# A buffer for single middle units, grouped plain copies and a TensorE turn of one weight tile in a fused attention and gated-MLP forward and backward pass

## The chip, the cores and the metric

The kernel runs on one core of a Trainium2 chip. A core has five engines with an instruction stream each: TensorE (PE, with its weight loads shown apart as PEld), VectorE (DVE), ScalarE (ACT), GpSimd (POOL) and SyncE (SP). SP does no arithmetic here. It issues most DMAs, in the order in which they stand in its stream. The metric is the time of one launch on the device, in microseconds, and less is better.

## The reference, cut to what matters

One layer mixes windowed attention and a gated MLP by a learned gate, and the kernel returns the output and the gradients for seven inputs (the eight outputs are out, dx, dwqkv, dwo, dW_gate, dW_up, dW_down and dgate_w).

```python
# S = 2048 rows, D = 512, 32 heads of 16, window 256, F = 1376, all bf16
g = sigmoid((x * gate_w).sum(-1, keepdims=True))
q, k, v = split_heads(x @ wqkv)
p = softmax(where(0 <= i - j < 256, q @ k.T * 16 ** -0.5, -1e9))
a = (p @ v) @ wo
gate, up = x @ W_gate, x @ W_up
b = (relu(gate) * up) @ W_down
out = g * a + (1 - g) * b
# and, for a given grad_out, d(out)/d(x, wqkv, wo, W_gate, W_up, W_down, gate_w)
```

## The kernel before, in words

The kernel has three stages. They follow each other on every engine, and the order of the instructions is written out by hand.

**Stage 1, the MLP (to about 250 us).** The 11 feature blocks (fc) of 128 columns and the 4 row groups (tg) of 512 rows give 44 steps, and the loop of line 410 runs them in a software pipeline. A step computes the gate, up and hidden-gradient products (L330), turns activations by DMA transposes on SP and accumulates weight gradients (L379, L381). The first steps also turn x (`turn_x`, L265) and the scaled output gradient (`turn_db`, L294) on TensorE, through the two PSUM slots with tag "tr". `WdT[fc]` is a tile of W_down, turned by a DMA transpose (`turn_wd`, L219). Its first tile is queued on SP behind the second quarter of x (`load_x(1)`) and ahead of the rest of x and grad_out (lines 243 to 252).

**Stage 2, attention (about 250 to 742 us).** The heads are taken in 4 groups of 8 (c = 0 to 3). A group goes through 16 rows (j) of 128 queries; a row is written (c,j) below. A row has a diagonal key block (role d), a middle one (m, keys of j-1) and a far one (f, keys of j-2). Each is done in two halves of four heads, so that a full row has six units. One unit is one step n of the loop of line 815:

- `front`: the scores ST (L626) on TensorE, the exponential into a bf16 tile on ACT (L635), a mask on POOL.
- `front_dp` and, a step later, `gradp`: the product dPT (L649), then a product on DVE (L654) into the second part of the same tile.
- three steps later, `rowsum`: the sums BA (L663, L665). After the row's last unit ACT copies them to `BAs` (L669, two buffers).
- `flip`: the probabilities are turned. For some units a DMA transpose on SP does it (L682, into p2d or p2m), for the others TensorE (L692).
- `cd_piece`: the products CD (L495, L498) for a key block, from the turned tiles and from `rq`. A list `cdq` holds them until a step that line 865 sets.
- `small_ops`: short POOL operations on `BAs` that make `rq` (five buffers) and, by way of a tile `t1`, the query gradient (L713 to L728).

The diagonal units are turned as a pair of halves from a tile PPd (three buffers). Middle units are turned by DMA as a pair in odd rows of groups 0 to 2. In even rows, and in rows 1 to 9 of group 3, it is a single: half 0 goes by DMA and half 1 by TensorE. Pairs and singles both take their tile from PPm, which has two buffers. In group 3 there are no middle pairs.

```python
u.pair = u.role == "d" or (u.role == "m" and j % 2 == 1 and c < DC - 1)
u.dma = u.pair or (u.role == "m" and half == 0 and (c < DC - 1 or j < 10))
```

Beside the rows, other work is fitted in by a running credit: the projections of the next 512 rows (`project_parts`, L128, L131), the weight gradients of the group before (`grad_parts`, L581), whose results are stored on SP two steps later (L574), and DMA transposes of weights for stage 3 (`turn_w`, L526). `spread` (L477) copies a projected tile zT into `zt` in four DMAs of 64 KB, two at each of two steps, and `tr_rows` (L171) turns zT by DMA. `spill` (L509) writes finished rows of q, k, v and output gradients to DRAM, 8 rows (1 MB) at a time.

**Stage 3, output and dx (742 us to the end).** For each of 16 row blocks TensorE forms the output and dx (L952, L956, L983, L998) and dwo (L933). Operands for two blocks at a time are loaded on SP.

Of the kernel before, what the change touches and what calls it, by code (L numbers as in the profile page):

```python
# [9 lines left out]
ALU = mybir.AluOpType  # L10
AX = mybir.AxisListType
BF = mybir.dt.bfloat16
F32 = mybir.dt.float32
# [9 lines left out]
def kernel(  # L23
# [20 lines left out]
    nc = tc.nc  # L44
# [143 lines left out]
    with ExitStack() as p1, tc.manual_schedule():  # L188
# [28 lines left out]
        def turn_wd(fc):  # L217
            WdT[fc] = fp.tile([P, DC, P], BF, tag="WdT", bufs=2, name="WdT")
            nc.sync.dma_start_transpose(out=WdT[fc][:], in_=B_W_down[start_of(fc):start_of(fc) + P, :])  # L219

        warm = fp.tile([P, TGW], BF, tag="rg", name="warm")
        nc.vector.memset(warm[:], 0.0)
        half = TPG // 2
# [17 lines left out]
            nc.sync.dma_start(Wu_sb[:, :, a:b], Wu_v[:, :, a:b])  # L241

        load_x(1)
        turn_wd(0)
        load_go(0)
        load_x(2)
        load_go(1)
        load_x(3)
# [161 lines left out]
        for n in range(N1 + 8):  # L410
            at = lambda lag: steps[n - lag] if 0 <= n - lag < N1 else None
            if at(0):
                gate(at(0))
                if n + 1 < NTG:
                    turn_x(n + 1)
                up(at(0))
                if n < NTG:
                    gate_col(n)
                    db_rows(n)
                if at(0).tg == 0 and at(0).fc > 0:  # L420
                    turn_wd(at(0).fc)
            if 1 <= n <= NTG:
                turn_db(n - 1)
            if at(2):
                dh(at(2))
            if at(1):
                turn_h(at(1))
            if at(3):
                keep(at(3), (hT_d, at(3).hT[:]))
            if at(4):  # L430
                turn_dgu(at(4))
                keep(at(4), (dgT_d, at(4).dgT), (duT_d, at(4).duT))
            if at(6):
                f = weights(at(6))
                if f is not None:
                    stores[n + 1] = f
            if n in stores:
                stores.pop(n)()
            t = n - DA0
            if t % 2 == 1 and 0 <= t // 2 < NT:  # L440
                make_da(t // 2)
            if t % 2 == 0 and 0 < t // 2 <= NT:
                turn_da(t // 2 - 1)
            if t == 2:
                nc.vector.reduce_sum(par[:, 0:1], par4[:], axis=AX.X)
                nc.vector.tensor_scalar(par[:, 1:2], par[:, 0:1], -1.0, 1.0, op0=ALU.mult, op1=ALU.add)
            if n == NTG + 1:
                nc.scalar.activation(tiny[:], tiny[:], ACT.Exp)
            if t in (NT + 3, 2 * NT + 1):
                i = (t - NT - 3) // (NT - 2)  # L450
                nc.gpsimd.memset(zt[i][:, 0, :, :, :], 0.0)
                nc.vector.memset(zt[i][:, 1, :, :, :], 0.0)
            if n == N1 - 2:
                first = project_parts(*groups[0])
            for _ in range({N1 + 1: 2, N1 + 2: 0}.get(n, 1)):
                if first:
                    first.pop(0)()
            z = n - DA0 - NT - 2
            if z == 0:
                load_w(0)  # L460
            if z % 4 == 3 and 0 < z // 4 + 1 < DC:
                load_w(z // 4 + 1)

    p3 = ctx
    if True:
# [21 lines left out]
        def cd_piece(c, kb, qb, half, last):  # L487
            if (c, kb) not in CDs:
                CDs[(c, kb)] = [ps.tile([P, HG, 2 * Dh], F32, tag="CD", bufs=1, name="CD"), True]
            cd = CDs[(c, kb)]  # L490
            rq = RQ[(c, qb)]
            p2 = P2[(c, qb, kb, half)]
            for hh in range(HH):
                h = 2 * hh + half
                nc.tensor.matmul(cd[0][:, h, :], lhsT=p2[:, 0, hh, :], rhs=rq[:, h, 0:2 * Dh],  # L495
                                 start=cd[1], stop=True, skip_group_check=True)
                cd[1] = False
                nc.tensor.matmul(cd[0][:, h, 0:Dh], lhsT=p2[:, 1, hh, :], rhs=rq[:, h, 2 * Dh:3 * Dh],  # L498
                                 start=False, stop=True, skip_group_check=True)
            if last:  # L500
                nc.scalar.copy(sts[c][:, kb, 1:3, :].rearrange("p a (h d) -> p h a d", h=HG),
                               cd[0][:].rearrange("p h (a d) -> p h a d", a=2))
                if kb == NT // 2 - 1 or (kb == NT - 1 and c == DC - 1):
                    spill(c, kb + 1 - NT // 2)

        def spill(c, t0):
            tsl = slice(t0, t0 + NT // 2)
            eng = nc.gpsimd if (c == DC - 1 and t0 > 0) else nc.sync
            eng.dma_start(dqkvo_d[t0 * P:(t0 + NT // 2) * P, c * 4 * P:(c + 1) * 4 * P].rearrange("(t p) n -> p t n", p=P),  # L509
                          sts[c][:, tsl, :, :].rearrange("p t a n -> p t (a n)"))  # L510

        S2 = {}
        nfull = F // P
# [106 lines left out]
        def front(u):  # L620
            tg, jl = u.j // TPG, u.j % TPG
            z = zt[(u.c * NTG + tg) % ZB]
            KTt = proj[(u.c, u.kb // TPG)][f"K{u.half}"]
            ksl = slice((u.kb % TPG) * P, (u.kb % TPG + 1) * P)
            ST = ps.tile([P, HH, P], F32, tag="M", bufs=4, name="ST")
            nc.tensor.matmul(ST[:], lhsT=KTt[:, ksl], rhs=z[:, 0, :, jl, :], start=True, stop=True)  # L626
            if u.dma:
                if u.half == 0:
                    pairs[(u.c, u.j, u.kb)] = wk.tile([P, 2, 2, HH, P], BF, tag=f"PP{u.role}",
                                                      bufs={"d": 3, "m": 2}[u.role], name=f"PP{u.role}")  # L630
                u.PP = pairs[(u.c, u.j, u.kb)][:, u.half, :, :, :]
                u.Pu, u.Pd = u.PP[:, 0, :, :], u.PP[:, 1, :, :]
            else:
                u.Pu = wk.tile([P, HH, P], BF, tag="Pu", bufs=3, name="Pu")
            nc.scalar.activation(u.Pu[:], ST[:], ACT.Exp)  # L635
            if u.role == "d":
                nc.gpsimd.affine_select(out=u.Pu[:], in_=u.Pu[:], compare_op=ALU.is_ge, fill=0.0, base=0,  # L637
                                        pattern=[[0, HH], [1, P]], channel_multiplier=-1)
            elif u.role == "f":
                nc.gpsimd.affine_select(out=u.Pu[:], in_=u.Pu[:], compare_op=ALU.is_ge, fill=0.0, base=-1,  # L640
                                        pattern=[[0, HH], [-1, P]], channel_multiplier=1)
# [55 lines left out]
        def small_ops(c, j, s):  # L697
# [4 lines left out]
            hd = lambda a: a.rearrange("p (h d) -> p h d", h=HG)  # L702
            rinv = wk.tile([P, HG], F32, tag="rinv", name="rinv")
            ndel = wk.tile([P, HG], F32, tag="ndel", name="ndel")
            rq = wk.tile([P, HG, 3 * Dh], BF, tag="rq", bufs=5, name="rq")
            t1 = wk.tile([P, HG, Dh], F32, tag="t1", name="t1")
            RQ[(c, j)] = rq

            def dve():
# [11 lines left out]
                nc.gpsimd.tensor_tensor(out=hd(rows_st[:, j, 3, :]), in0=BAs[:, :, 17:33], in1=bc(rinv[:], Dh), op=ALU.mult)  # L721

            def pool3():
                nc.gpsimd.tensor_tensor(out=t1[:], in0=BAs[:, :, 0:16], in1=bc(ndel[:], Dh), op=ALU.mult)
                nc.gpsimd.tensor_tensor(out=t1[:], in0=t1[:], in1=BAs[:, :, 34:50], op=ALU.add)

            def pool4():
                nc.gpsimd.tensor_tensor(out=hd(rows_st[:, j, 0, :]), in0=t1[:], in1=bc(rinv[:], Dh), op=ALU.mult)  # L728

            at = (6, 7, 10, 12) if j == 0 else (4, 5, 6, 7)  # L730
            return ((s + 3, "dve", dve),) + tuple((s + a, "pool", f) for a, f in zip(at, (pool1, pool2, pool3, pool4)))
# [54 lines left out]
        with tc.manual_schedule():  # L786
# [14 lines left out]
            def background():  # L801
                f, more = bgq.pop(0)
                store = f()
                if store is not None:
                    ev.setdefault(n + 2, []).append(("dma", store))
                return more

            def pieces():
                nonlocal credit
# [5 lines left out]
            while n <= NU + LAG or ev or cdq or bgq:  # L815
                now = ev.pop(n, [])
                u = units[n] if n < NU else None
                if u is not None:
# [3 lines left out]
                    if u.first and u.j % TPG == 0:  # L822
                        if gi + 1 < len(groups):
                            prq = project_parts(*groups[gi + 1])
                            due = n + sum(2 * min(3, j + 1) for j in range(u.j, u.j + TPG)) - 3
                            if gi + 2 == len(groups):
                                due -= 10
                    if u.first and u.j == 6 and u.c > 0:
                        ev.setdefault(n + 1, []).append(("dma", lambda c=u.c - 1: spill(c, NT // 2)))
                    if u.first and u.j == 1 and u.c > 0:  # L830
                        ready = grad_parts(u.c - 1)
                    if u.first and u.j == TPG - 1 and u.c > 0:
# [18 lines left out]
                if w is not None:  # L851
# [3 lines left out]
                    if w.last:  # L855
# [5 lines left out]
                        for kb in done:  # L861
                            qbs = range(kb, min(NT, kb + 3))
                            for qb in qbs:
                                for half in range(2):
                                    e = n + 1 if qb < w.j else n + 5
                                    cdq.append((e, w.c, kb, qb, half, qb == qbs[-1] and half == 1))
                if u is not None and not (w is not None and w.first):
                    front_dp(u)
# [13 lines left out]
                elif prq and not held and ((credit > 0.4 and n > fed + 1) or due - n <= len(prq)):  # L882
# [2 lines left out]
                    prq.pop(0)()  # L885
                    if len(prq) == 4:
                        for k in range(NP):
                            ev.setdefault(n + 1 + k // 2, []).append(("dma", lambda gi=gi, k=k: spread(gi + 1, k)))
                    if not prq:
                        late += plan.get(gi + 1, [])  # L890
                elif bgq and len(prq) <= 2 and credit > 0.3:
# [149 lines left out]
```

## Time and profile before

| quantity | value |
|---|---|
| times of three runs | 934.29, 937.22 and 938.29 us, median 937.22 |
| the profiled execution | 937.59 us, its span 935.9 us |
| TensorE busy | 910.8 us, 97% of the span |
| VectorE, ScalarE, GpSimd busy | 489.4, 446.6 and 482.7 us, 52%, 48% and 52% |
| granted TensorE clock | 0.998 |
| SP's hardware queue q1 | 142.10 MB, 80.6% of 16 engines' span |
| spills | 7 of 1024 KB on SP, 5.8 us to landing, and one on POOL |
| DMA transposes of probabilities | 64 into p2d (5.5 us to landing), 54 into p2m (4.4 us) |

The profile lists, for each engine, its busy time, groups of instructions and what ended the idle time before them. A line such as "A <- B: 14.2, 11, 2.5" in the view of waits says that A waited for B 14.2 us in total, 11 times, 2.5 us at the longest. In a timeline the columns are start, duration, engine, line and operation, and a bracket at the end holds the idle time before it and what ended it. PE is idle for about 25 us of the span.

### The profile page before, as it was taken

The page shows a single profiled execution, that of the slowest core. Times are in us where ns is not written, and L with a number is a line of the kernel's source. Part 1 is how long each engine was busy: PE and PEld are TensorE (multiplying, and loading weights), DVE is VectorE, ACT ScalarE, POOL GpSimd, SP SyncE. Part 2 cuts the span into 40 slices and gives each one's busy share as a digit, 9 for nine tenths or more (in the row PEclk, how much of TensorE's full clock was granted, in tenths as well). Part 3 has the DMA queues.
Part 4 walks back from the last instruction along what each step waited for, and adds up shares of the span by engine and source line. Part 5 has one row for each costly group of instructions (what it writes and reads, how often), then busy time and mean ns, then how long its engine had stood idle before and what let it go on. Part 6 is the DMA issues. An engine that isn't in the chain of part 4 may idle for free.

```text
span 935.9 us, 26578 instructions
## 1 busy us (share of the span) xinstructions
PE 910.8 (97%) x10873; PEld 576.2 (62%) x10873; DVE 489.4 (52%) x910; ACT 446.6 (48%) x784; POOL 482.7 (52%) x934
## 2 busy tenths in 40 slices
PE   7999999999999999999999999999999999999998
PEld 4565656555657776677676677667777644444443
DVE  4433344333377777667676676766677322222223
ACT  5422232222368777567776677766688211111111
POOL 1554545445267777666677567666667411111111
PEclk9999999999999999999999999999999999999999
DMA  9988889999798999998999789999999599778731
GB/s 264 212 194 186 195 177 221 206 220 197 165 166 140 163 194 164 145 177 145 183 170 169 162 131 200 158 173 163 172 183 193 147 272 225 186 186 189 186 93 46
DMA packets 485043, 166.49 MB, mean 178 GB/s; under 512 B 409720, under 2 KB 483672, under 8 KB 484920
## 3 DMA queue, kind: packets, MB, share of 16 engines
q1 hardware_dynamic: 462568, 142.10, 80.6%
q10 hardware_dynamic: 20592, 17.57, 6.8%
q0 software_dynamic: 1760, 5.11, 1.6%
q8 instruction: 85, 1.39, 0.6%
q14 instruction: 38, 0.31, 0.1%
HBM read 32.15 MB, written 36.24 MB: 73 GB/s over the span
## 4 chain that ended last, share of the span: by engine, by line
PE 79%; DMA 7%; POOL 5%; ACT 5%; DVE 2%; issue 1%; SPq 0%; POOLq 0%; ACTq 0%; DVEq 0%
PE wps L379 8%; PE dxps L983 7%; PE ST L626 6%; PE dPT L649 6%; PE pt L692 5%; PE dxps L998 4%; DMA p2m<-PPm 4%; PE wps L581 4%; PE dps L381 4%; PE dhps L330 4%; PE ups L330 4%; PE gps L330 4%; PE bps L952 4%; PE CD L495 3%; PE pp L128 3%; PE BA L663 3%
## 5 line engine op out<-in xcount | busy, mean ns | idle before, releaser
L637 POOL TENSOR_SCALAR_AFFINE_SELECT PPd<-PPd 128x512 bf16<-128x512 bf16 x128 | 81.2, 634 | 128.9 <-ACT PPd L635 127.9
L654 DVE TENSOR_TENSOR Pd<-Pu,dPT 128x512 bf16<-128x512 bf16 x154 | 104.0, 679 | 73.4 <-POOL Pu L640 72.3
L626 PE MATMUL ST<-z,K 128*128 128x512 bf16 x360 | 136.5, 379 | 5.5 <-ACT PPm L635 3.3
L649 PE MATMUL dPT<-z,V 128*128 128x512 bf16 x360 | 136.9, 380 | 3.0 <-ACT PPm L635 2.1
L344 POOL TENSOR_TENSOR hT<-rg,upm 128x512 bf16<-128x512 bf16 x44 | 52.2, 1186 | 119.6 <-DVE upm L342 85.0
L635 ACT ACTIVATE Pu<-ST 128x512 bf16<-128x512 f32 x154 | 92.6, 601 | 43.8 <-PE ST L626 42.8
L379 PE MATMUL wps<-dgu_r,x_r 128*128 128x256 bf16 (+1 forms) x704 | 103.9, 270 | 0.5 <-DVE wst L74 0.5
L654 DVE TENSOR_TENSOR PPd<-PPd,dPT 128x512 bf16<-128x512 bf16 x128 | 87.3, 682 | 19.9 <-POOL PPd L637 18.0
L635 ACT ACTIVATE PPd<-ST 128x512 bf16<-128x512 f32 x128 | 77.3, 604 | 23.1 <-PE ST L626 20.6
L379 PEld LDWEIGHTS <-x_r 128*128 128x128 bf16 x704 | 68.3, 98 | 31.2 <-issue 0.8
L640 POOL TENSOR_SCALAR_AFFINE_SELECT Pu<-Pu 128x512 bf16<-128x512 bf16 x112 | 71.7, 640 | 22.3 <-ACT Pu L635 21.3
L961 ACT COPY a_sb<-aps 128x512 f32<-128x512 f32 x16 | 9.4, 586 | 152.9 <-issue 137.7
L342 DVE SCALAR_TENSOR_TENSOR upm<-rg,ups 128x512 bf16<-128x512 bf16 x44 | 30.2, 685 | 85.6 <-ACT rg L336 45.8
L336 ACT ACTIVATE rg<-gps 128x512 bf16<-128x512 f32 x44 | 26.3, 598 | 93.9 <-PE gps L330 22.0
L381 PE MATMUL dps<-db_r,h_r 128*128 128x512 bf16 x176 | 66.8, 379 | 0.0
L635 ACT ACTIVATE PPm<-ST 128x512 bf16<-128x512 f32 x78 | 47.1, 604 | 32.3 <-PE ST L626 15.9
L354 POOL TENSOR_TENSOR dgu<-dh_sb,rg 128x512 bf16<-128x512 bf16 x44 | 56.5, 1285 | 8.0 <-ACT dh_sb L350 7.0
L692 PE MATMUL pt<-ident,Pd 128*128 128x128 bf16 x616 | 59.9, 220 | 0.0
L692 PE MATMUL pt<-ident,Pu 128*128 128x128 bf16 x616 | 59.4, 218 | 0.0
L654 DVE TENSOR_TENSOR PPm<-PPm,dPT 128x512 bf16<-128x512 bf16 x78 | 52.6, 674 | 5.6 <-ACT PPm L635 4.3
L967 POOL DMA_DIRECT2D out_dram<-o_sb x16 | 8.7, 542 | 90.7 <-DVE o_sb L965 90.7
L72 ACT COPY p<-pt 128x1024 bf16<-128x1024 bf16 x51 | 52.4, 1028 | 1.3
(172 smaller groups left out, 2361.5 us busy)
## 6 DMA issues: line engine op xcount, KB each, us to landing
dqkvo_d<-rows_st SPq DMA_DIRECT2D x7, 1024.0 KB, 5.8
hT_d<-hT ACTq DMA_DIRECT2D x44, 128.0 KB, 2.5
dgT_d<-dgu ACTq DMA_DIRECT2D x44, 128.0 KB, 2.9
duT_d<-dgu ACTq DMA_DIRECT2D x44, 128.0 KB, 3.1
duT_g<-duT_d SPq DMA_DIRECT2D x8, 640.0 KB, 5.7
gt<-hT_d SPq DMA_DIRECT2D x7, 640.0 KB, 5.4
dgT_g<-dgT_d SPq DMA_DIRECT2D x7, 640.0 KB, 5.2
z<-zT SPq DMA_DIRECT2D x60, 64.0 KB, 2.2
```

What stands on the lines that cost most here:

```text
L330: nc.tensor.matmul(out[:], lhsT=w(c), rhs=x(c), start=(c == 0), stop=(c == DC - 1))
L354: nc.gpsimd.tensor_tensor(out=k.duT, in0=dh_sb[:], in1=k.rg[:], op=ALU.mult)
L379: nc.tensor.matmul(acc["w"][:, c, 0:2 * nw], lhsT=x_r[:, t, c * P:(c + 1) * P], rhs=k.dgu_r[:, :, i, s0:P], start=(go_ and c % 2 == 0), st ...
L381: nc.tensor.matmul(acc["d"][:], lhsT=k.h_r[:, i, :], rhs=db_r[:, t, :], start=go_, stop=no_)
L626: nc.tensor.matmul(ST[:], lhsT=KTt[:, ksl], rhs=z[:, 0, :, jl, :], start=True, stop=True)
L635: nc.scalar.activation(u.Pu[:], ST[:], ACT.Exp)
L637: nc.gpsimd.affine_select(out=u.Pu[:], in_=u.Pu[:], compare_op=ALU.is_ge, fill=0.0, base=0, pattern=[[0, HH], [1, P]], channel_multiplier=-1)
L640: nc.gpsimd.affine_select(out=u.Pu[:], in_=u.Pu[:], compare_op=ALU.is_ge, fill=0.0, base=-1, pattern=[[0, HH], [-1, P]], channel_multiplier=1)
L649: nc.tensor.matmul(u.dPT[:], lhsT=VTt[:, ksl], rhs=z[:, 1, :, jl, :], start=True, stop=True)
L654: nc.vector.tensor_tensor(out=u.Pd[:], in0=u.Pu[:], in1=u.dPT[:], op=ALU.mult)
L692: nc.tensor.transpose(pt[:, a, hh, :], src[:, hh, :], ident[:])
L983: nc.tensor.matmul(dxps[:], lhsT=src[:, fc, lsl], rhs=W6[(wt, fc)], start=(i == 0), stop=(i == nmm - 1))
```

## The change

- **Singles.** Middle pairs keep PPm with its two buffers. A middle single takes a tile of half the size with a tag of its own, PPs, which has one buffer, in all four head groups.
- **Room for it.** `t1` goes away: the query gradient is formed in place in `BAs`, so a `BAs` buffer is held until the last POOL operation of its row. `rq` has four buffers instead of five.
- **Plain copies.** The four copies of `spread` are issued at one step. Stores of weight gradients and spills wait in a list `copies` until more than two are there or until the copies of `spread` have been issued, and then go out together. Spills are of 4 rows (512 KB). In head group 3 a spill goes out at once, and the very last one on POOL's queue.
- **CD.** In rows 9 to 15 of head group 3 the last pieces of a key block are due six steps after the row's sums, not five.
- **First W_down tile.** Tile 0 of W_down is loaded by a plain DMA behind the first quarter of grad_out, turned by four TensorE transposes into a "tr" slot in step 1 and copied out by DVE. The DMA transpose ahead of grad_out is gone.

```diff
+        wd0 = fp.tile([P, D], BF, tag="dst", bufs=2, name="wd0")
+        def turn_wd0():
+            WdT[0] = fp.tile([P, DC, P], BF, tag="WdT", bufs=2, name="WdT")
+            pt = ps1.tile([P, DC, 2, P], BF, tag="tr", bufs=2, name="ptw")
+            for c in range(DC):
+                nc.tensor.transpose(pt[:, c, 0, :], wd0[:, c * P:(c + 1) * P], ident[:])
+            nc.vector.tensor_copy(WdT[0][:], pt[:, :, 0, :])
...
         load_x(1)
-        turn_wd(0)
         load_go(0)
+        nc.sync.dma_start(wd0[:], B_W_down[0:P, :])
...
+                if n == 1:
+                    turn_wd0()
             if 1 <= n <= NTG:
                 turn_db(n - 1)
...
-                if kb == NT // 2 - 1 or (kb == NT - 1 and c == DC - 1):
-                    spill(c, kb + 1 - NT // 2)
+                if kb % TPG == TPG - 1:
+                    sp = lambda: spill(c, kb + 1 - TPG)
+                    if c == DC - 1:
+                        sp()
+                    elif kb < NT - 1:
+                        copies.append(sp)
+                    else:
+                        ends.append(sp)
...
-                    pairs[(u.c, u.j, u.kb)] = wk.tile([P, 2, 2, HH, P], BF, tag=f"PP{u.role}",
-                                                      bufs={"d": 3, "m": 2}[u.role], name=f"PP{u.role}")
+                    nh, tag, bufs = (2, f"PP{u.role}", {"d": 3, "m": 2}[u.role]) if u.pair else (1, "PPs", 1)
+                    pairs[(u.c, u.j, u.kb)] = wk.tile([P, nh, 2, HH, P], BF, tag=tag, bufs=bufs, name=tag)
...
-            rq = wk.tile([P, HG, 3 * Dh], BF, tag="rq", bufs=5, name="rq")
-            t1 = wk.tile([P, HG, Dh], F32, tag="t1", name="t1")
+            rq = wk.tile([P, HG, 3 * Dh], BF, tag="rq", bufs=4, name="rq")
...
-                nc.gpsimd.tensor_tensor(out=t1[:], in0=t1[:], in1=BAs[:, :, 34:50], op=ALU.add)
+                nc.gpsimd.tensor_tensor(out=BAs[:, :, 0:16], in0=BAs[:, :, 0:16], in1=BAs[:, :, 34:50], op=ALU.add)
...
-                    ev.setdefault(n + 2, []).append(("dma", store))
+                    copies.append(store)
+                    if len(copies) > 2 or gi + 2 >= len(groups):
+                        ev.setdefault(n + 2, []).append(("dma", flush))
...
+            def flush():
+                while copies:
+                    copies.pop(0)()
...
-                    if u.first and u.j == 6 and u.c > 0:
-                        ev.setdefault(n + 1, []).append(("dma", lambda c=u.c - 1: spill(c, NT // 2)))
+                    if u.first and u.j == TPG and ends:
+                        copies.append(ends.pop(0))
...
-                                    e = n + 1 if qb < w.j else n + 5
+                                    e = n + (1 if qb < w.j else 6 if w.c == DC - 1 and w.j > 8 else 5)
...
-                            ev.setdefault(n + 1 + k // 2, []).append(("dma", lambda gi=gi, k=k: spread(gi + 1, k)))
+                            ev.setdefault(n + 1, []).append(("dma", lambda gi=gi, k=k: spread(gi + 1, k)))
+                        ev.setdefault(n + 1, []).append(("dma", flush))
```

In SP's stream of the changed kernel, head group 3 begins with p2d (2,15), p2d (3,0), four copies z, a spill of 512 KB, the single p2m (3,1), rows, p2d (3,1) and p2m (3,2). Before it was p2d (2,15), p2d (3,0), two copies z, p2m (3,1), rows, two copies z, p2d (3,1), p2m (3,2).

## The prediction

> **What bounds the kernel now.** I read the page first, for the engine that sets the end.
>
> ```profile
> span 935.9 us, 26578 instructions
> PE 910.8 (97%) x10873; PEld 576.2 (62%) x10873; DVE 489.4 (52%) x910; ACT 446.6 (48%) x784; POOL 482.7 (52%) x934
> DMA  9988889999798999998999789999999599778731
> ```
>
> TensorE works through 910.8 of 935.9 us at full clock, and the edits take no matmul from it. So what can be won is idle time of PE, 25.1 us, of which the ends of the launch hold several. What can be lost has no such limit. The third line says where a loss could come from: the DMA engines are nine tenths busy through most of attention (slices 11 to 31).
>
> Second, the view of waits for PE, over attention to 560 us, from there to 690 us, from 690 to 760 us, and before 245 us.
>
> ```profile
> PE ST L626 <- ACT PPm L635: 3.1, 3, 2.0
> PE wps L581 <- ACT PPm L635: 1.3, 1, 1.3
> ```
> ```profile
> PE dPT L649 <- ACT PPm L635: 2.1, 2, 1.8
> PE ST L626 <- ACT PPd L635: 0.9, 1, 0.9
> PE ST L626 <- ACT PPm L635: 0.2, 1, 0.2
> ```
> ```profile
> PE CD L495 <- POOL rq L719: 2.6, 6, 0.9
> PE dxps L983 <- DMA duT_g<-duT_d: 0.6, 1, 0.6
> ```
> ```profile
> PE ptx L265 <- DMA x_r<-in_A_x_dram: 2.4, 2, 1.6
> PE ptx L265 <- DVE db_T L74: 0.9, 1, 0.9
> ```
>
> These are the targets: 4.4 us up to 560 us and 2.3 us after it behind the middle exponential, 2.6 us behind `rq`, 2.4 us behind x at the start. Third, the same view for ACT over the whole run says what holds the exponential, and it is a DMA that must first read the old tile.
>
> ```profile
> ACT PPm L635 <- DMA p2m<-PPm: 14.2, 11, 2.5
> ```
>
> ACT waits 14.2 us in 11 waits and PE idles 6.7 us for it. So about 0.7 us of each such wait is absorbed by PE's lead.
>
> Fourth, the timelines of ACT and of SP in head group 3, and the landing of the single issued at 618.51.
>
> ```profile
> 613.70 0.60 ACT L635 ACTIVATE PPm<-ST 128x512 bf16<-128x512 f32 x1 [0.37 <-PE BA L665]
> 622.93 0.60 ACT L635 ACTIVATE PPm<-ST 128x512 bf16<-128x512 f32 x1 [0.23 <-PE ST L626]
> ```
> ```profile
> 611.89 4.45 SPq L682 DMA_TRANSPOSE p2d<-PPd  x2
> 616.44 1.98 SPq L477 DMA_DIRECT2D z<-zT  x2
> 618.51 1.28 SPq L682 DMA_TRANSPOSE p2m<-PPm  x1
> ```
> ```profile
> DMA to landing us min/median/max: 3.3/3.3/3.3
> ```
>
> The first two lines are the exponentials that open rows (3,2) and (3,3). The single of row (3,1) is issued at 618.51 and lands 3.3 us later, at 621.8, which is 8.1 us after (3,2) has opened. With two buffers that harms nobody. With one buffer, (3,2) may not open before 621.8.
>
> Last, the view of DMA queues from 560 to 622 us, to see if that landing could come sooner.
>
> ```profile
> DMA packets 39854, 11.23 MB, mean 181 GB/s; under 512 B 38433, under 2 KB 39841, under 8 KB 39841
> q1 hardware_dynamic: 39841, 11.06, 109.4%
> ```
>
> SP's queue holds all 16 engines for the whole of these 62 us (packets overlap, hence 109%). It is full, and it moves 11.06 MB / 62 us = 0.178 MB per us.
>
> **The change part by part.** All sums are against the profiled execution, 937.59 us (span 935.9 and 1.7 around it), which lies 0.4 us above the median of 937.22.
>
> *Pairs keep PPm.* A pair is reused four rows later instead of two. Rows take 6 to 10 us and a p2m lands 8.9 us after issue at worst, so these waits go. Up to 560 us that is 4.4 us off PE.
>
> *Singles in groups 0 to 2.* One buffer reused two rows later is the distance of before: no cost. Their landings come 2 to 10 us before the reuse in nearly all rows, and one wait of 0.4 us (1,12) stays.
>
> *Singles in group 3.* Here a single is made in every row, so the distance falls from two rows to one. In a full queue the landing of p2m (3,1) is set by the bytes ahead of it. Between 560 us and that landing, before has one spill of 1 MB and after has two of 512 KB, and after has two more z copies ahead: 0.13 MB / 0.178 = 0.7 us. So it lands at 622.5, less the shift of all that came earlier, and (3,2) opens then instead of at 613.70: 8.8 us later. PE's lead absorbs 0.7, and PE's wait behind PPd (0.9, at 618) does not come on top, which leaves 7.2. The 2.3 us of PPm waits after 560 us vanish in this: whatever PE gains there it waits out here. Grouping may let the queue switch less between copies and transposes. No row prices that. Between 0 and 2 us I take 1, by the landing of z, z, rows, z, z at 583.6 to 590.2, where 0.5 MB take longer than the 2.8 us of the mean rate. So +6.2 us, with ends of +2 and +9. Behind the blocked exponential on ACT stand the copies of turned tiles, of BA and of CD. PE runs on only until its four score slots are taken, so it stops within two units.
>
> *Rows (3,3) to (3,9).* In before, singles land 4.7, 2.8, 3.6, 2.3 and 0.7 us after the opening of the next row in rows 3, 4, 5, 6 and 8. But that is the backlog, and the long wait works it off: a row needs p2d, p2m and two weight turns, 40 tiles of 32 KB or 1.3 MB, 7.4 us of queue in rows of 9.3 us. What remains are rows with copies in front of the single. At (3,5) two stores, a spill, p2d, four z and rows stand ahead of it. I take +2, between 0 and +6.
>
> *CD one step later.* Five of the six waits for `rq` are in rows 10 to 14 (0.24 four times and 0.69), the last is in the drain. A step is 1.2 us, more than any of them: -1.7 (ends 0 and -2.6).
>
> *The place of t1.* `BAs` of row 0 is now held to its last POOL operation. In group 2 that ends at 504.3 (L728), while ACT copies `BAs` of row 2 at 503.1. ACT waits 1.2 us, and PE, whose next BA stood at 504.56, sees at least 0.2 and at most 1.2 us. Three groups (the fourth is inside the long wait): +1.0. `rq` with four buffers: a buffer is read until two rows later, so it is free in time, 0.
>
> *First W_down tile.* The windows of DMA show 45 GB/s between 8.0 and 9.5 us, when the transpose is under way, and 326 GB/s right after it:
>
> ```profile
> 8.00:9.50 1.50, 0.72 (x13) 0.72 (x14) 0.06 (x1) 0.60 (x1) 0.00 (x0) 1.00 1.27 45
> 9.50:17.00 7.50, 5.94 (x85) 4.05 (x83) 4.59 (x9) 4.81 (x8) 1.81 (x2) 1.00 1.05 326
> ```
>
> Without it x and grad_out land some 2 us sooner, and the 2.4 us behind x go. Added are four transposes of 0.07 us on PE (16 take 1.07) and one copy on DVE of about 0.45 us (128x512 from PSUM takes 0.40 to 0.48), and the second turn of the first output gradient needs the slot that this copy frees. The copy stands behind two scalings (1.53 us), so PE waits there for more than the 0.9 us that it waited for db_T. I take -1.5, between -2.4 and +0.3.
>
> *Other copies.* The last spill is 512 KB on POOL's queue instead of 1 MB, so duT_g comes earlier: -0.6. On SP a group of copies takes 0.6 us each to issue, 3 us in a row; except in group 3 they have two rows of slack.
>
> The Trainium skill's page "DMA: Bandwidth & Descriptors", section "Rules for kernel authors", speaks against smaller spills: it wants at least 1 MiB per DMA for bandwidth, and calls transfers under 64 KB mostly overhead. The rows here half agree: 640 KB land in 5.2 to 5.7 us and 1024 KB in 5.8. If a half spill held the full queue as long as a whole one, the sum would be some 3 us higher; by bytes it is as above.
>
> Sum: -4.4 + 6.2 + 2 - 1.7 + 1.0 - 1.5 - 0.6 = +1.0. That is 938.6 against the profiled execution, 938.2 on the scale of the median, and I forecast 938.
>
> **The rivals.** *The single buffer holds every row (slower).* The queue doesn't recover, because p2m (3,j) always stands behind p2d (3,j-1) and two weight turns. For it: the five landings above, late by 14.1 us in all. Five waits less 0.7 us each give 10.6 instead of 2: 947. Against it: the queue's demand of 7.4 us a row. It decides from about 6 us of waits after (3,2), where the total passes 941.9. That half spills hold the queue like whole ones leads to the same place, 941.
>
> *The queue runs ahead (faster).* If grouped copies spare the queue 2 us per group, three groups before p2m (3,1) bring it 6 us forward instead of 1, and the long wait shrinks to about 1 us: 933; with no waits after it, 931. For it: within the 62 us slices fall to 61 to 86 GB/s between slices of 290. Against it: nothing shows that the switch is what empties them.
>
> *The start wins nothing*, since DVE's copy takes the place of the wait: 939.5, still no change.
>
> **How the numbers follow.** A measurement of this kernel can tell about 0.5%, 4.7 us, from no change. My sum has 0.40, and its own range is 934 to 942. The slower rival has 0.34 and the faster one 0.26. These are also the chances of the three signs: faster 0.26, same 0.40, slower 0.34. For 8 times in 10 the range is 930 to 948.
>
> **What would show it.** In the changed kernel: no wait of ACT for p2m<-PPm worth naming; one wait of ACT for p2m<-PPs of 8 to 13 us near 605 to 618 us, with PE idle for most of it; no wait for `rq` in rows 10 to 14; x no longer waited for at 12 us. The prediction is wrong if PE has no hole at the opening of (3,2), or if PPs waits follow in most rows of group 3 and add up to over 6 us.

## The result, and the profile after

Six executions of the changed kernel took 946.43 to 950.21 us, median 947.23; the kernel before took 935.75 in the same comparison. The ratio is 1.0129, 95% interval 1.0100 to 1.0158: slower by 1.3%. It lies inside the stated range of 930 to 948, at its upper end, where the slower rival stood (947). The forecast of 938 was 9.2 us too low, and the sign was wrong with it: 0.40 had been given to no change and 0.34 to slower.

The profiled execution took 946.43 us, 8.84 more than that of before. It is the fastest of its six, and that of before (937.59) lies near the top of its range (932.97 to 938.33), so the two traces hold 8.8 of the 11.5 us between the medians. The page's heads, its row for TensorE and its row of granted clock:

```profile
span 944.7 us, 26622 instructions
PE 912.2 (97%) x10877; PEld 576.7 (61%) x10877; DVE 492.6 (52%) x911; ACT 448.8 (48%) x784; POOL 481.9 (51%) x934
PE   8999999999999999999999999689999899999998
PEclk9999999999999999999999999889999999999999
```

TensorE is busy 912.2 us instead of 910.8, and the clock has two digits of 8 (slices 26 and 27), where before it had none below 9. (A digit stands for 23 us, and a short stretch at half clock can hide in a 9: before has one, shown further down.) The hole is the 6 of TensorE's row, slice 26, 590 to 614 us. The view of waits for TensorE from 560 to 690 us, and for ACT in the same stretch, name it:

```profile
PE dPT L667 <- ACT PPs L653: 13.6, 3, 10.2
```
```profile
ACT PPs L653 <- DMA p2m<-PPs: 20.2, 4, 12.1
```

The waits for PPm (4.4 and 2.3 us of TensorE before) are gone. One wait of 10.2 us stands in their place, and two more of 2.8 and 0.6. The timeline of ACT shows the two long ones, at the opening of rows (3,2) and (3,3):

```profile
615.07 0.60 ACT L653 ACTIVATE PPs<-ST 128x512 bf16<-128x512 f32 x1 [12.08 <-DMA p2m<-PPs]
627.56 0.60 ACT L653 ACTIVATE PPs<-ST 128x512 bf16<-128x512 f32 x1 [4.50 <-DMA p2m<-PPs]
```

The timeline of SP shows what stands ahead of the single of row (3,1), issued at 611.04. It lands 4.0 us later, at 615.0, and there the exponential starts:

```profile
601.51 6.15 SPq L700 DMA_TRANSPOSE p2d<-PPd  x2
607.75 2.54 SPq L488 DMA_DIRECT2D z<-zT  x4
610.34 0.59 SPq L527 DMA_DIRECT2D dqkvo_d<-rows_st  x1
611.04 1.71 SPq L700 DMA_TRANSPOSE p2m<-PPs  x1
```

**Where the time went.** The 360 dPT products (L649 before, L667 after) stand in the same order in both timelines, so subtracting their starts gives TensorE's lead or lag at each unit.

| at the product of | before, us | after, us | difference | change since the row above |
|---|---|---|---|---|
| first unit of attention | 251.52 | 248.99 | -2.53 | -2.53 |
| opening of (2,11) | 567.21 | 560.35 | -6.87 | -4.34 |
| opening of (3,2) | 613.54 | 603.21 | -10.34 | -3.47 |
| two units later | 616.52 | 617.22 | +0.70 | +11.04 |
| opening of (3,3) | 623.38 | 623.75 | +0.37 | -0.33 |
| near the end of (3,3) | 629.88 | 634.72 | +4.84 | +4.47 |
| last unit of (3,6) | 658.85 | 664.91 | +6.06 | +1.22 |
| opening of (3,11) | 692.95 | 699.01 | +6.06 | 0.00 |
| last unit of all | 728.26 | 736.76 | +8.50 | +2.44 |
| end of the span | 935.87 | 944.73 | +8.86 | +0.36 |

So TensorE was first 10.3 us ahead. It lost 16.4 in rows (3,2) to (3,6), and another 2.4 in the last rows. Not all of the lead is the change's: the version with two buffers below has the same start and came to attention at 251.52 us, no sooner than before.

**The clock.** Idle TensorE does not explain all of the 16.4. The view of windows, with the stretches cut at the ends of the two holes (after the engines' busy times come granted clock, DMA share and GB/s):

```profile
605.50:608.50 3.00, 0.00 (x0) 0.00 (x0) 0.00 (x0) 0.00 (x0) 0.00 (x0) 1.00 1.14 132
608.50:615.70 7.20, 0.00 (x0) 0.00 (x0) 0.00 (x0) 0.63 (x2) 0.00 (x0) 0.52 0.90 208
615.70:618.80 3.10, 3.08 (x38) 1.70 (x38) 2.40 (x5) 2.37 (x5) 1.94 (x5) 0.50 0.00 0
618.80:625.40 6.60, 6.58 (x120) 4.81 (x119) 4.57 (x10) 3.52 (x6) 5.39 (x16) 0.98 0.89 103
628.20:629.60 1.40, 1.40 (x15) 0.90 (x15) 0.67 (x1) 0.79 (x3) 0.61 (x2) 0.88 1.19 215
629.60:632.70 3.10, 3.10 (x19) 1.83 (x17) 1.49 (x3) 1.93 (x3) 1.40 (x4) 0.50 0.84 157
```

The clock falls to half 3.3 us after TensorE stopped (605.5) and stays there until 3.3 us after it took up work again (615.7). After the second hole (625.4 to 628.2) it falls again, for another 3.4 us (629.3 to 632.7). In these stretches a dPT product takes 586 to 634 ns instead of 378. Half of 3.3 and of 3.4 us, 3.3 us in all, is lost on top of the idle time. With the waits of 13.6 and 0.3 us, and less the 0.9 that before waited at 618 us, that makes 16.3 of the 16.4. The Trainium skill's page "TensorE: Matmul & The Clock Gate", section "Part 1: The HAM clock gate (the "warmup" mystery)", says that the array runs at half rate after an idle window of about 3.4 us and recovers after a busy one of that length, by a window that runs freely. The stretches of 3.3 and 3.4 us here agree. That the whole window must be idle does not hold here: the second hole lasted 2.8 us (see the last section).

### The profile page after: what moved, and what is told of

Its sections match the earlier page's. It is cut to its first block, busy times and chain, and to the rows that moved or that the text cites. A ratio compares the mean times of both kernels' runs of the same rounds, so it can differ in the third digit from the quotient of the medians.

```text
span 944.7 us, 26622 instructions
## 1 busy us (share of the span) xinstructions
PE 912.2 (97%) x10877; PEld 576.7 (61%) x10877; DVE 492.6 (52%) x911; ACT 448.8 (48%) x784; POOL 481.9 (51%) x934
## 4 chain that ended last, share of the span: by engine, by line
PE 82%; POOL 5%; ACT 4%; DMA 3%; DVE 2%; issue 2%; SPq 1%; POOLq 0%; ACTq 0%; DVEq 0%
PE wps L388 8%; PE dxps L1007 8%; PE ST L644 7%; PE dPT L667 6%; PE pt L710 5%; PE dxps L1022 4%; PE wps L599 4%; PE dhps L339 4%; PE dps L390 4%; PE ups L339 4%; PE gps L339 4%; PE bps L976 4%; PE pp L128 4%; PE CD L506 3%; PE BA L681 3%; PE CD L509 2%
## 5 line engine op out<-in xcount | busy, mean ns | idle before, releaser
L667 PE MATMUL dPT<-z,V 128*128 128x512 bf16 x360 | 136.8, 380 | 14.6 <-ACT PPs L653 13.6
L681 PE MATMUL BA<-KV,Pu 128*128 128x33 bf16 x616 | 51.1, 178 | 0.5 <-POOL Pu L658 0.5
L599 PE MATMUL wps<-rows_st,x_r 128*128 128x384 bf16 x256 | 50.8, 328 | 0.3 <-DVE Pd L672 0.3
```

Source lines behind the costliest of these rows:

```text
L599: nc.tensor.matmul(wps[:], lhsT=x_r[:, t, part * P:(part + 1) * P], rhs=sts[c][:, t, 0:3, :], start=first and t == t0, stop=last and t == ...
L667: nc.tensor.matmul(u.dPT[:], lhsT=VTt[:, ksl], rhs=z[:, 1, :, jl, :], start=True, stop=True)
L681: nc.tensor.matmul(BA[:, h, 0:33], lhsT=u.Pu[:, hh, :], rhs=kv[:, u.kb % TPG, h, 1:34], start=(u.first and hh == 0), stop=True, skip_group ...
```

## Experiments

Ratios are to the kernel before, run in the same comparison. Versions that ran in different comparisons are set against each other by their ratios. The changed kernel itself has 1.0129 (1.0100 to 1.0158).

**Two buffers for the singles of head group 3.**

```diff
-  nh, tag, bufs = (2, f"PP{u.role}", {"d": 3, "m": 2}[u.role]) if u.pair else (1, "PPs", 1)
+  nh, tag, bufs = (2, f"PP{u.role}", {"d": 3, "m": 2}[u.role]) if u.pair or u.c == DC - 1 else (1, "PPs", 1)
```

> The changed kernel, except that singles of head group 3 take their tile from PPm (two buffers, which no pair needs in that group) and no longer from PPs (one buffer). Groups 0 to 2 are as changed. Theory A, the one buffer makes the long wait, and the wait makes the slow clock behind it: no wait of ACT for p2m in head group 3 worth naming, no idle time of TensorE over 2 us between 600 and 660 us, granted clock 1.00 there. TensorE, which in the changed kernel is 10.3 us ahead of the kernel before at the opening of row (3,2), keeps about 9.4 us of that (it then waits 0.9 us for p2d as before), loses the 2.8 us that the changed kernel loses from row (3,10) on, and ends 6 to 7 us ahead: 929 to 930 us, ratio to before 0.993. Rival B, SP's queue is late for everything in this stretch and the wait moves to PPd or to the CD products: 937 to 942 us. Rival C, the wait is not due to the buffer: 947 us as the changed kernel.

Measured: 936.84 us, ratio 1.0019 (1.0003 to 1.0035). The second buffer takes off 1.1% of the 1.3, but the 929 to 930 us did not come. The hole of row (3,2) is gone. Another one stands at the opening of row (3,3), which now waits for the same single of row (3,1):

```profile
PE ST L644 <- ACT PPm L653: 3.8, 1, 3.8
```
```profile
ACT PPm L653 <- DMA p2m<-PPm: 5.1, 1, 5.1
```

It lands at 619.2 (issue 612.62, 6.6 us), and with the slow clock (0.66 from 620 to 625 us) the hole costs 5.5 us. (The profiled execution, 939.01 us, is the slowest of twelve, so the trace shows the worst case.) So the single buffer is the cause of most of the loss (theory A), and under it lies a second limit: with the queue as it is, a TensorE 8 us ahead has no landing in time even with two buffers. The time fell between A and B, at the edge of B.

**CD at five steps again.**

```diff
-  e = n + (1 if qb < w.j else 6 if w.c == DC - 1 and w.j > 8 else 5)
+  e = n + 1 if qb < w.j else n + 5
```

> The changed kernel with the CD products of the last rows of head group 3 five steps after the row's sums, as before, and not six. By the prediction the later step takes 1.7 us of waits for rq away, so that undoing it gives 949 us and the waits for rq of 0.24 us in rows 10 to 14 come back. Rival, by the trace of the changed kernel, in which TensorE falls 2.8 us behind from row (3,10) on and waits for the products of DVE (0.59 us four times and 1.05 once): the later CD causes these, and undoing it gives 944.5 us.

Measured: 944.98 us, ratio 1.0111 (1.0086 to 1.0136). The medians differ by 2.2 us, but the intervals overlap; the trace is clearer, though it is of the slowest of the four executions (948.21 us, 3.7 us later than the changed kernel when attention begins). From row (3,11) to the last unit TensorE loses nothing against the kernel before, where the changed kernel loses 2.4 us. The view of waits for TensorE from 690 to 760 us, first of the changed kernel, then of this one:

```profile
PE ST L644 <- DVE Pd L672: 3.4, 5, 1.0
```
```profile
PE CD L506 <- POOL rq L736: 2.6, 6, 0.9
```

The later CD does remove the waits for `rq`, as predicted. But no other work takes the place of the CD products that leave the step, so TensorE comes to the next score product earlier and waits there for the slot that a DVE product frees: 3.4 us, and 1.0 more in the drain, instead of 2.6. The rival holds.

**The first W_down tile by DMA again.**

```diff
+        turn_wd(0)
         load_go(0)
-        nc.sync.dma_start(wd0[:], B_W_down[0:P, :])
...
-                if n == 1:
-                    turn_wd0()
```

> The changed kernel with the first W_down tile turned by the DMA transpose of before. Theory A, the end of the long wait is set by SP's queue and not by TensorE: TensorE comes to attention about 2 us later, the wait at the opening of row (3,2) is 2 us shorter, p2m (3,1) lands at the same 615.0 us within 0.7, and the time is the changed kernel's 947.2 within 1 us. Rival B, the queue starts what it does as TensorE releases it, so everything shifts: p2m (3,1) lands 2 us later and the time is 949.3 us.

Measured: 948.03 us, ratio 1.0140 (1.0114 to 1.0166), the changed kernel's time. TensorE comes to attention 1.0 us later, is 0.7 us later at row (3,2), and the hole is 10.1 us. What the old start cost, 1.0 us, is less than two executions of one kernel differ by, so this run does not decide between A and B. The trace of the version above, with CD at five steps, does: its stream is the same up to row (3,9), TensorE is 3.8 us later at row (3,2), the single is issued 3.7 us later (614.72), and the hole is still 10.2 us. The queue's work moves with TensorE's, as B has it.

**Copies, stores and spills ungrouped.** `spread`, the stores and the spills of 1 MB are issued where the kernel before has them; the single buffer stays.

> The changed kernel with the copies of projected tiles, the stores of weight gradients and the spills issued as before (two and two copies, each store two steps after its piece, spills of 1 MB). The single buffer stays. Theory A, the bytes ahead of p2m (3,1) set the end of the long wait: two copies less stand ahead of it, so it lands 0.4 to 1 us sooner, the wait stays at 10 to 12 us, and the time is 946 to 948 us. Rival B, the four copies and the half spill that grouping puts ahead of p2m (3,1) make the wait: it lands 3 us or more sooner, the wait is under 9 us, 944 us or less. Rival C, grouping had brought the queue forward: it lands 2 us or more later, 949 us or more.

Measured: 947.80 us, ratio 1.0138 (1.0115 to 1.0161). The single lands at 617.2 instead of 615.0, of which 1.5 us lie in a later start of attention. TensorE's hole there is 7.2 us, after one of 2.2 us on PPd a row earlier, which brought a slow clock of its own (half from 605.95 to 609.36 us). From the opening of (3,1) to that of (3,4) TensorE loses 14.8 us here and 15.0 in the changed kernel. The time is A's; neither B nor C: the grouping did not make the loss, and it did not bring the landing forward by the 6 us that the faster rival of the prediction needed.

**Weight transposes held back, single buffer kept.**

```diff
+                wait = u is not None and (u.c, u.j) > (DC - 2, 11) and (u.c, u.j) < (DC - 1, 4)
-                if late and (u is None or n % 3 == 1):
+                if late and not wait and (u is None or n % 3 == 1):
```

> The changed kernel, single buffer and all, but no DMA transpose of a stage 3 weight is issued from row (2,12) to row (3,3); the four that stood there, and those behind them, follow from row (3,4) on. In the trace of the changed kernel with two singles these four take SP's queue 6.3 us to issue (1.24, 1.53, 2.18 and 1.31 us). Theory A, the backlog of SP's queue sets the end of the long wait: p2m (3,1) lands 5 to 6 us sooner, at 609 to 610 us, TensorE's hole at the opening of row (3,2) falls from 10.2 to 4 to 5 us, the slow clock behind it goes in part: 938 to 941 us. Rival B, the wait is set by the chain of p2d (2,15), p2d (3,0), the copies and the single, each as long as it is: the hole shrinks by 2 us at most, 945 us. Rival C, the turns that come later make waits of their own in rows 4 to 9: 947 us or more.

Measured: 949.40 us, ratio 1.0161 (1.0132 to 1.0189). The queue has room now: SP issues p2m (2,15) at 596.3, 2.7 us earlier than in the changed kernel, and stands idle in between. The wait stays all the same. The timeline of SP:

```profile
597.82 6.84 SPq L700 DMA_TRANSPOSE p2d<-PPd  x2
604.71 2.91 SPq L488 DMA_DIRECT2D z<-zT  x4
607.66 1.39 SPq L527 DMA_DIRECT2D dqkvo_d<-rows_st  x1
609.17 1.68 SPq L700 DMA_TRANSPOSE p2m<-PPs  x1
```

The single's product is finished at 603.2, but it stands behind the p2d of row (3,0), four copies and a spill, and lands at 613.2, 1.8 us sooner than in the changed kernel. The hole is 6.6 us instead of 10.2, and half of that difference comes from TensorE being 1.7 us later there. That is B for the landing. Rows (3,3), (3,6) and (3,8) bring waits of 2.4, 2.8 and 0.9 us, where the changed kernel has 2.8, 0.6 and none: that is C for the time. (The intervals of the two ratios overlap, so it is no slower than the changed kernel for certain.) With one buffer a row apart, a full queue isn't needed: the order in it is enough.

**All three edits together, and two of them.** Two buffers, CD at five steps, weight transposes held back; then the same without holding them back.

> Three edits to the changed kernel at once: singles of head group 3 from PPm (two buffers), CD in the last rows five steps after the sums, and no weight transposes from row (2,12) to row (3,3). Theory A, the wait of 5.1 us at the opening of row (3,3) with two buffers is the backlog of SP's queue: it goes, TensorE keeps 8 to 10 us of its lead to row (3,10) and to the end, no slow clock: 926 to 929 us, ratio 0.990 to 0.993. Rival B, the transposes held back return as waits in rows 4 to 9 or as late operands of stage 3: 932 to 936 us, a hole of 2 us or more between 630 and 760 us.

> The version with three edits without the third: two buffers for the singles of head group 3, CD at five steps, weight transposes where the changed kernel has them. If the edits add up, the 2.2 us that CD at five steps gave the changed kernel come off the 936.8 us of the version with two buffers alone: 934.6 us, and the hole of 3.9 us at the opening of row (3,3) with its slow clock is there. Then holding the transposes back is worth 8 us on top of the second buffer. Rival: the hole moves with chance by the order in SP's queue, 928 to 931 us.

Measured: 926.45 us, ratio 0.9908 (0.9886 to 0.9930), and 932.43 us, ratio 0.9970 (0.9957 to 0.9983). Both beat both kernels. The page of the first, and a line of its view of waits for ACT:

```profile
span 925.0 us, 26520 instructions
PEclk9999999999999999999999999999999999999999
```
```profile
ACT PPm L653 <- DMA p2m<-PPm: 1.5, 1, 1.5
```

TensorE is 9.3 us ahead of the kernel before at row (3,2), 10.1 at row (3,11) and 10.9 at the end. Without holding back, the hole at (3,3) is 2.9 us, the clock is at half from 619.8 to 623.2 us, and the lead falls from 8.8 to 4.3 us. Holding the transposes back is worth 0.62% (5.8 us, not the 8 expected) with two buffers and nothing with one. The 932.43 us lie between the two expectations of that version.

**Held back in the kernel before, alone.**

> The kernel before with only one edit: no weight transposes from row (2,12) to row (3,3). Theory A, from row (2,13) on the middle exponentials of before wait because SP's queue is late, and not because PPm is short: the waits of TensorE after 590 us (1.8, 0.28, 0.92 and 0.2 us) go, 932 to 933 us, ratio 0.996 to 0.997. Rival B, they are due to the buffer or to the row's own transposes alone: no change, 935.5 us.

Measured: 931.84 us, ratio 0.9968 (0.9953 to 0.9983), as theory A said. The waits of 1.8, 0.28, 0.92 and 0.2 us after 590 us are gone, those of 2.1, 1.3 and 0.5 us up to 560 us stay. So the last ones came from a late queue. The earlier ones are gone in the changed kernel, where pairs have PPm to themselves: they came from the short PPm. What the rest of the change adds, with two buffers and CD at five steps, is the difference to 0.9908, 0.6%.

**Rows (3,1) and (3,2) turned on TensorE, with CD at five steps.** The edit beside that of CD:

```diff
-  u.dma = u.pair or (u.role == "m" and half == 0 and (c < DC - 1 or j < 10))
+  u.dma = u.pair or (u.role == "m" and half == 0 and (c < DC - 1 or 2 < j < 10))
```

> The changed kernel with CD at five steps, and with the middle units of rows (3,1) and (3,2) turned on TensorE as in rows 10 to 15, so that the first single of head group 3 is that of row (3,3). The single buffer stays, and so do the weight transposes. Theory A: the hole at the opening of row (3,2) goes. TensorE does 16 transposes more (0.5 to 1 us for each of two units). If the queue is still late, row (3,4) waits for p2m (3,3) by 1 to 5 us: 929 to 934 us. Rival B, PPd takes its place, since p2d of rows 15 and 0 is in the same queue: waits of ACT for p2d of 3 us or more at rows (3,2) or (3,3), 936 us or more.

Measured: 931.90 us, ratio 0.9980 (0.9961 to 0.9999), against 1.0111 with CD at five steps alone. No hole of 0.4 us or more is left between 560 and 690 us, though the single buffer is in use from row 3 on. ACT still waits 4.9 us for p2m in two waits, little enough for TensorE's lead to absorb most. Its profiled execution is the fastest of ten (928.51), so the trace shows the best case.

**Useless work in the holes.**

```diff
+        FILL = {(DC - 1, 2, "f", 0): 130, (DC - 1, 3, "f", 0): 30}
...
+            m = FILL.get((u.c, u.j, u.role, u.half))
+            if m:
+                pf = psr.tile([P, 2, HH, P], BF, tag="TR", name="pf")
+                for i in range(m):
+                    nc.tensor.transpose(pf[:, i % 2, i // 2 % HH, :], ident[:], ident[:])
```

> The changed kernel with useless TensorE transposes of the identity put into its two holes, 130 ahead of the dPT product that waits 10.2 us in row (3,2) and 30 ahead of the one that waits 2.8 us in row (3,3). At 16 in 1.07 us they take about 8.7 and 2.0 us, less than the holes, so they delay nothing if the holes are as long. Theory A, the idle time itself brings the slow clock (0.5 for about 3.7 us from 615.3 us on, and again from 629.4 to 632.6 us): the granted clock stays 1.00 through both, and TensorE is 2 to 3.5 us earlier at row (3,4) for the same landing of p2m (3,1): 944 to 945 us. Rival B, the clock falls for another reason: no change or, by the added work, 947 to 949 us.

Measured: 951.92 us, ratio 1.0167 (1.0135 to 1.0200). The 130 transposes took 7 us and left a hole of 4.4, after which the clock fell all the same (0.74 from 622.4 to 629 us). Around the second place 0.8 us of idle time was left, the clock stayed at 1.00, and TensorE made up 1.9 us against the changed kernel. So the second half of theory A is borne out, the first was not tried long enough. Why the median is 4.7 us above the changed kernel's stays open. In the trace, which is of the slowest of the four executions, 4.7 us were already missing when attention began, before any of this work: 2.1 of them are a wait for a DVE copy that ends at 203.3 us, and 1.7 the half clock behind it, from 203.2 to 206.6 us. So the total says little about either theory.

**What grouping and the new start are worth without the hole.** The version with all three edits, once ungrouped, once with the old start.

> The version with three edits (two buffers for the singles of head group 3, CD at five steps, weight transposes held back), with copies, stores and spills issued as before. It tells what the grouping is worth when no long wait covers it. Theory A, the grouping moves bytes a little and saves nothing: 926 to 928 us, ratio 0.990 to 0.992. Rival B, the grouping is what keeps the waits behind p2m away: waits of ACT for p2m of 3 us or more come back, 930 us or more. Rival C, the grouped copies cost: 924 us or less.

> The version with three edits, with the first W_down tile turned by DMA as before. It tells what the turn on TensorE is worth when no long wait covers it. By the prediction 1.5 us: 928 us. Rival, by the trace of the changed kernel with the old start, in which TensorE came to attention 1.0 us later: 927.4 us. Rival, nothing, since the wait for the DVE copy of 1.6 us takes the place of those removed: 926.4 us.

Measured: 928.64 us, ratio 0.9933 (0.9913 to 0.9954), and 926.50 us, ratio 0.9908 (0.9888 to 0.9928). The grouping seems to win about 2 us: the ratios 0.9933 and 0.9908 have overlapping intervals, but in one comparison the six executions with it (and the old start) end at 927.08 us and the six without begin at 927.58. None of the three expectations had that. In the traces of the ungrouped version and the one with all three edits, attention is alike to 0.6 us; 2.2 us appear only after its last unit, where the granted clock of the ungrouped one is 0.68 from 720 to 725 us and that of the other 1.00. Whether the grouping or chance sets that off stays open. The new start shows no worth (0.9908 with either start).

## Why the prediction was right or wrong

The trace came out at +8.9 us where the sum had +1.0. Of these 7.9 us, 4.1 lie in the term for CD, 3.7 in that for rows (3,3) to (3,9), 1.0 in the long wait and 1.0 in stage 3; the terms up to 560 us came out 2.0 better than forecast.

- *Pairs keep PPm, -4.4.* Right, but low. After 560 us the lead grows by 3.5, where 2.3 were expected; as predicted, that went into the hole. To (2,11) it grows by 4.3 us against a loss of 1.3 to `BAs`, so 5.7. What the sum lacks is a slow clock in the kernel before: its longest wait for PPm, 1.97 us up to 268.3, is followed by 3.4 us at half clock, and with the wait that goes too (1.7 us). The windows of before:

```profile
265.19:268.60 3.41, 1.44 (x23) 0.92 (x22) 2.75 (x6) 0.86 (x2) 3.21 (x10) 1.00 1.28 148
268.60:272.01 3.41, 3.41 (x32) 2.04 (x31) 1.72 (x4) 2.69 (x5) 2.29 (x5) 0.50 1.16 225
```
- *The long wait, +6.2.* Right, and closely. By the terms of the sum TensorE should have been 1.3 us behind the kernel before when the hole was over (-4.4, -1.5, +1.0, +6.2); at the opening of (3,3) it was 0.4 behind. The single landed at 615.0, where 622.5 less the shift of 4.9 and the 1 us for grouping gives 616.6. That the two ends meet so well is partly luck: TensorE came to row (2,11) 2.0 us further ahead than the sum has it, and from there to (3,3) lost 7.2 us and not 6.2.
- *Rows (3,3) to (3,9), +2.* This step failed. From the opening of (3,3) to row (3,11) TensorE lost 5.7 us. The waits were 2.8 and 0.6 us, not far above the expected sum: the long wait did work the backlog off, so the slower rival's five waits did not come, though its time did. What was missing is the clock, 1.7 us in these rows and as much in the work just before them. The prediction reads TensorE as running "at full clock" from a mean of 0.998; the two lines above, of a hole of 2 us in the kernel before, show the slow clock that a hole of 8 us had to be priced with.
- *CD one step later, -1.7.* Wrong in sign, and the largest miss: +2.4 by the trace. The wait for `rq` did go, but I named no work that would fill its place and did not ask what TensorE would wait for next.
- *The place of t1, +1.0.* The sum was nearly right: ACT has three waits, 2.4 us in all, of which TensorE felt only the first, 1.3 us at 266 us. So the size came from one wait and not from three. Waits of TensorE from 245 to 560 us:

```profile
PE BA L681 <- ACT BAs L687: 1.3, 1, 1.3
```

- *First W_down tile, -1.5.* Wrong. The rival "the start wins nothing" is what the old start in the version with all three edits shows (ratio 0.9908 with either). The wait for x shrinks from 2.4 to 0.9 us, and TensorE waits 1.6 us for the DVE copy. Even the smaller wait for x is in part chance: it is 0.8 and 1.1 us in the two traces with the old start, and 0.4 to 1.8 in those with the new one. Waits of TensorE before 245 us:

```profile
PE ptd L303 <- DVE WdT L228: 1.6, 1, 1.6
PE ptx L274 <- DMA x_r<-in_A_x_dram: 0.9, 2, 0.6
```

- *Other copies, -0.6.* The wait for duT_g is gone, but the end of the kernel came 0.4 us later relative to the last unit, not sooner. Half spills took 3.4 us to landing (154 GB/s) and whole ones 5.8 (181 GB/s), so a half did not take as long as a whole one. The whole ones moved faster, which agrees with the rule of at least 1 MiB in the Trainium skill's page "DMA: Bandwidth & Descriptors", section "Rules for kernel authors". No run here shows that the smaller ones cost time.
- *The rivals.* "The single buffer holds every row" gave the right time by half the right mechanism: the single buffer, but one long wait, the clock and the later CD, not five waits. That the time lies in the range is luck to that extent: the range was wide for another reason. "The queue runs ahead" did not happen: ungrouping moved the single's landing by less than 1 us relative to attention.
- *The signs.* Most came: ACT waits once for 12.1 us, no wait for p2m<-PPm or `rq` is left in the rows named, and TensorE has its hole. For x it still waits 0.2 us before 11.7 us. ACT's later waits for PPs add up to 8.1 us (4.5, 2.9 and 0.7), over the 6 that were named, but in three rows and not in most; TensorE felt 3.4 of them.

## What to carry to other kernels

A buffer is short or long by the distance between two uses at the place where that distance is smallest: one tile for singles was enough in three head groups and cost 10 us in the first rows of the fourth, where a single is made every row and stands in an in-order queue behind other copies. Price a hole in TensorE's work as its length and then some: behind holes of 2 us and more the clock of most ran at half for 3.4 us, which costs up to 1.7 us. And if a wait is removed by moving work behind it, name what fills the place, or the engine only arrives at its next wait sooner.

## What the runs showed of the hardware

In each of the fourteen traces the clock changes only at points of a grid with a step of 3.41 us. In the changed kernel these are 608.79, 619.03, 629.27 and 632.69 us, which lie 3, 3 and 1 steps apart. By all fourteen, what decides is how long TensorE is idle within one step (its idle time as the view of windows gives it). Every step with 1.96 us or more of idle time was followed by one at half clock, none with less than 0.9 us was, and in between both occurred. So a hole need not last as long as a step, and its place decides. One of 2.8 us in the changed kernel put 2.35 us into the step that ends at 629.27, and brought the slow clock 1.1 us after work had begun again. One of 2.9 us in the ungrouped version fell across two steps, 1.5 and 1.3 us in each, and brought none. The two steps:

```profile
626.43:629.84 3.41, 1.90 (x30) 1.33 (x28) 1.45 (x3) 0.00 (x0) 2.57 (x7) 1.00 1.09 126
629.84:633.25 3.41, 2.07 (x24) 1.42 (x24) 1.31 (x2) 2.16 (x5) 1.13 (x3) 1.00 1.18 205
```

The same clock explains some of the scatter between executions. Of the 17 executions of the kernel before that ran beside the version with two buffers, the five with a mean clock of 1.000 took 932.4 to 933.8 us and the four with 0.996 took 935.3 to 937.6; the eight with 0.998 took 933.0 to 938.0. With small waits only, the clock fell to 0.66 and 0.76 from 15 to 20 us in two profiled executions (two buffers; CD at five steps), which came to attention 2.5 and 3.7 us later than the changed kernel with the same start. In six, a step at half clock begins between 741 and 754 us, after the last unit.

Inside the long hole, with the copies not yet issued (the first at 607.75 us), the transposes of p2d moved 101 and 64 GB/s from 606 to 608 us and 290 in the microsecond after. The busy share of the DMA engines was 1.95 in the first of these microseconds and 0.32 in the second. No experiment here tells what slowed the first and emptied the second.
